# Attention and spectral mixing on one core: v of chunks 28 and 29 made batch by batch, and TensorE's work at the end put into its waits for weights

## The chip, the core and the metric

The kernel runs on one core of a Trainium2 chip. The time is the device time of one execution in microseconds (us); before the change the median of three runs was 439.15 us. Five engines work side by side, each through its own list of instructions in order: TensorE (PE in the profile), VectorE (DVE), ScalarE (ACT), GpSimd (POOL) and SyncE (SP). They wait for each other through semaphores. DMAs are issued by GpSimd's and SyncE's queues and carried by 16 DMA engines.

## The reference

Two stages. First, causal attention over 8 batches, 8 heads, 576 positions and 64 features, with a bias from a running sum. Its result is `x`, 8 x 576 x 512. Then a spectral mix of `x`, cut to its core:

```
X = rfft(x, axis=1)
Xr, Xi = X.real[:, :64], X.imag[:, :64]
Yr = einsum('bmd,mde->bme', Xr, w_r) - einsum('bmd,mde->bme', Xi, w_i)
Yi = einsum('bmd,mde->bme', Xr, w_i) + einsum('bmd,mde->bme', Xi, w_r)
y = irfft(Yr + 1j * Yi, n=576, axis=1)
u = x + y
out = u + maximum(u @ w_ch, 0)
```

`w_r` and `w_i` hold 64 matrices of 512 x 512 each in float32: 134 MB together, all read once.

## The kernel before

The weights are read in 32 **chunks**, four groups of 128 input features (`g`) by eight blocks of eight modes (`c`). A chunk has a real and an imaginary half, `ri` 0 and 1, and each half is one buffer of 128 x 8 x 512 in bfloat16, filled by two DMAs that cast on the way. The last half, the imaginary one of chunk 31, comes in four smaller pieces. GpSimd issues these DMAs (L245), far ahead of their use, as soon as a buffer is free. At most eight of its DMAs are under way.

The first 24 chunks are multiplied between the steps of the attention, the last eight (group 3, chunks 24 to 31, `c` = 0 to 7) behind it. In that last part the code is one straight list, and every engine works through it in the order in which it is written. Nothing reorders it.

- `modes(g, c)` (L479) multiplies one chunk: eight matmuls with the real weights, eight with the imaginary ones. With `meanwhile={2: f}` it calls `f` between the two halves, so that other work of TensorE stands there. For group 3 VectorE adds the sum of the earlier groups (L503) and leaves `yb`: 128 rows (8 modes, real and imaginary, of 8 batches), 512 columns.
- `y_transposed` (L696, copy on ScalarE L698) transposes `yb`; `y_times_wch` (L704, cast on VectorE L708) multiplies it with `w_ch` and leaves `vb`, which is `v = Y @ w_ch`.
- `yv` holds `y` and `v` for the inverse transform, modes on the partitions, batches apart. `spread` (L514) moves the rows of one chunk there with a DMA on SyncE's queue, 128 KB within the core's memory. `gather_round` (L721) does it without a DMA: matmuls that take one batch's columns from the transposed `y` (`which` 0: times the identity, gives `y`; `which` 1: times `w_ch`, gives `v`), and copies from PSUM into `yv` (L732), on ScalarE for `v` and on VectorE for `y` unless said otherwise.
- `work` does the next of the early products of `x` with `w_ch`: `x_transposed` (L663, copies L667) of a pair of output tiles, and `keep` (L676), which multiplies the pair transposed before and has ScalarE put the result aside (L536). `late[-1]` is the last such pair, number 17.
- `x_times_wch` (L676) begins the sums `z` of pairs 0 and 1, `add_y` (L764) and `add_last` (L775) add the inverse transforms to them, `first_u` (L794) begins `u` of pair 0. `add_y(..., slice(0, GK))` reads `yv` of chunks 24 to 29, `add_last` takes chunks 30 and 31 as they come.
- Behind chunk 31 the list of steps from L943 on makes the outputs: sums, ReLU on ScalarE, additions on VectorE and GpSimd, and 20 DMAs to `out`.

In the part that the change touches, TensorE's order before is: chunk 27; three rounds of the gather for chunks 24 to 27 with a `work` behind the third, the fourth round, the last `keep` of a `work`; chunk 28, its transposes, its `v`; chunk 29's real half, its imaginary half, the transposes of `x` for pairs 17 and 0, the transposes of `y`, `z` of pair 0, the transposes of `x` for pair 1, `v`, the gather of `y` for chunks 28 and 29; chunk 30's real half, `keep` of pair 17, its imaginary half, `z` of pair 1 with the transposes of `y` between, `v`; `z` of pair 0 with `yv`; chunk 31.

PSUM has eight banks of 128 x 512 float32: four for `z`, two in `upool` (for the transposes of `x` and a part of the gather, later for `u` of pair 0), two in `auxpool` (for `modes`, the transposes of `y`, `v` and the rest of the gather).

Of the kernel before, what the change touches and what calls it, by code (L numbers as in the profile page):

```python
# [19 lines left out]
def kernel(  # L20
# [20 lines left out]
    NG = DM // P  # L41
# [6 lines left out]
    NCK = NM // MC  # L48
# [207 lines left out]
    for n in range(N):  # L256
# [4 lines left out]
        while nt < min(w // 2, len(wq)):  # L261
            i = ring_of(nt)
# [208 lines left out]
    def modes(g, c, meanwhile=None):  # L471


        ps = auxpool.tile([P, DM], FP32, name="yp", tag="aux")
        cols = xs[g % 2].rearrange("p q k h r b m -> p q k (h r b) m")

        def product(ri, q_, cg):
            k0 = HP if ri == 1 and c == 0 and cg == 0 else 0
            nc.tensor.matmul(  # L479
                ps[32 * cg : 32 * cg + 32, :],  # L480
                cols[k0:, q_, 1 - ri, :, c * MC // 2 + cg],
                wt[(g, c, ri)][cg // 2][k0:, 2 * (cg % 2) + q_, :],
                start=(ri == 0 and q_ == 0), stop=(ri == 1 and q_ == 1),
                tile_position=(k0, 32 * cg), skip_group_check=True,
            )

        for x in range(4):
            ri, y = divmod(x, 2)
            if meanwhile and x in meanwhile:
                meanwhile[x]()  # L490
            for z in range(4):
                if meanwhile:
                    product(ri, z // 2, 2 * y + z % 2)
                else:
                    product(ri, y, z)
        if g == 0:
            nc.vector.tensor_copy(out=y_acc[:, c, :], in_=ps)
        elif g < NG - 1:
            nc.vector.tensor_tensor(out=y_acc[:, c, :], in0=ps, in1=y_acc[:, c, :], op=ALU.add)  # L499
        else:  # L500
            yb = spool.tile([P, DM], FP16, name="y_sb", tag="y")
            for cols in halves if c == NCK - 1 else [slice(0, DM)]:
                nc.vector.tensor_tensor(  # L503
                    out=yb[:, cols], in0=ps[:, cols], in1=y_acc[:, c, cols], op=ALU.add
                )
            if c >= NCK - 1:
                spread(c, 0, yb)
            return yb
# [140 lines left out]
    xts, zs = {}, {}  # L649
# [7 lines left out]
    def x_transposed(i):  # L657
        xts[i] = xt_sb[len(xts) % 3]
        for x, (b, T) in enumerate(pairs[i]):
            ps = upool.tile([P, DT, P], FP32, name="xt_ps", tag="u")  # L660
            for rows, bb, ident in parts(b, T):
                for dt in range(DT):
                    nc.tensor.matmul(  # L663
                        ps[:, dt, rows], x_all[: rows.stop - rows.start, dt, bb, T, :],
                        ident, start=True, stop=True, skip_group_check=True,
                    )
            nc.vector.tensor_copy(out=xts[i][:, x], in_=ps)  # L667
# [4 lines left out]
    def x_times_wch(i, last, xx=(0, 1)):  # L672
        for x in xx:
            start_z(i, x)
            for dt in range(DT):
                nc.tensor.matmul(  # L676
                    zs[i, x], xts[i][:, x, dt, :], wch_sb[:, dt, :],
                    start=(dt == 0), stop=(last and dt == DT - 1), skip_group_check=True,
                )

    def keep(i):
        x_times_wch(i, True)
        j = late.index(i)
        kept_place(i, places[j])
        for x in range(2):
            keep_product(i, x, zs.pop((i, x)))
# [3 lines left out]
    NY = NCK // 2  # L690
    yt_first = finpool.tile([P, DT, NY, P], FP16, name="yt_first")

    def y_transposed(yb, c=NCK):
        ps = auxpool.tile([P, DT, P], FP16, name="yt_ps", tag="aux")
        for dt in range(DT):
            nc.tensor.transpose(ps[:, dt, :], yb[:, bass.ts(dt, P)], ident16h)  # L696
        yt = yt_first[:, :, c % NY, :] if c < NCK - 2 else spool.tile([P, DT, P], FP16, name="yt_sb", tag="yt")
        nc.scalar.copy(out=yt, in_=ps)  # L698
        return yt

    def y_times_wch(c, yt):
        vp = auxpool.tile([P, DM], FP32, name="v_ps", tag="aux")
        for dt in range(DT):
            nc.tensor.matmul(  # L704
                vp, yt[:, dt, :], wch_sb[:, dt, :], start=(dt == 0), stop=(dt == DT - 1)
            )
        vb = spool.tile([P, DM], FP16, name="v_sb", tag="v")
        nc.vector.tensor_copy(out=vb, in_=vp)  # L708
        if c < NCK - 2:
            spread(c, 1, vb)  # L710
        return vb

    def gather_round(c0, c1, b0, which, pool):

        n = 2 * MC * (c1 - c0)
        ng = P // n
        ps = pool.tile([P, DM], FP32, name="g_ps", tag="u" if pool is upool else "aux")
        for dt in range(DT):
            op = yt_first[:, dt, c0 % NY : c0 % NY + c1 - c0].rearrange("p c (x b) -> p (c x) b", b=B)
            for g in range(ng):  # L720
                nc.tensor.matmul(  # L721
                    ps[n * g : n * g + n, :] if which else ps[n * g : n * g + n, bass.ts(dt, P)],
                    op[:, :, b0 + g],
                    wch_sb[:, dt, :] if which else ident16h,
                    start=(dt == 0 or not which), stop=(dt == DT - 1 or not which),
                    tile_position=(0, n * g), skip_group_check=True,
                )

        def copies(engine=None):
            copy = {"v": nc.vector.tensor_copy, "s": nc.scalar.copy}[engine or ("s" if which else "v")]  # L730
            for g in range(ng):
                copy(out=yv[2 * MC * c0 : 2 * MC * c1, b0 + g, which, :], in_=ps[n * g : n * g + n, :])  # L732

        return copies
# [3 lines left out]
    def work():  # L738

        if not order_z and not ahead:  # L740
            return
        if order_z:
            i = order_z.pop(0)
            x_transposed(i)
            ahead.append(i)
        if len(ahead) == 2 or not order_z:
            i = ahead.pop(0)
            keep(i)
# [8 lines left out]
    GK = P - 2 * MC * NX  # L757

    def add_y(dst, i, which, rows=slice(0, P), start=False, xx=(0, 1)):

        for x in xx:
            b, T = pairs[i][x]
            for r, bb, _ in parts(b, T):
                nc.tensor.matmul(  # L764
                    dst[x][r, :], G_sb[rows, bass.ds(T * P, r.stop - r.start)],
                    yv[rows, bb, which, :], start=start, stop=True, skip_group_check=True,
                    tile_position=(0, r.start),
                )

    def add_last(dst, i, yb, cols=slice(0, DM), c=NX - 1, xx=(0, 1)):  # L770

        for x in xx:
            b, T = pairs[i][x]
            for r, bb, _ in parts(b, T):
                nc.tensor.matmul(  # L775
                    dst[x][r, cols], Gx_sb[:, c, bass.ts(T, P)] if T < NF else Gt_sb[:, bb, c], yb[:, cols],
                    start=False, stop=True, skip_group_check=True, tile_position=(0, r.start),
                )
# [64 lines left out]
    def z_of(i):  # L843
        return [zs[i, x] for x in range(2)]

    for c in range(NCK - 2):
        yb = modes(NG - 1, c)
        for x in range(TAKE[c] - 1):
            work()
        if c == NCK - 3:  # L850
            x_transposed(late[-1])
            x_transposed(0)
        yt = y_transposed(yb, c)
        if TAKE[c]:
            work()
        if c >= NY:
            if c == NCK - 3:
                x_times_wch(0, False)
                x_transposed(1)
            y_times_wch(c, yt)  # L860
            if c == NCK - 3:
                for x in range(2):
                    gather_round(NY, NCK - 2, 4 * x, 0, upool)("sv"[x])
        elif c == NY - 1:
            for x, pool in enumerate((auxpool, upool, auxpool, auxpool)):
                for which in (1, 0):
                    gather_round(0, NY, 2 * x, which, pool)()
                if x >= 2:
                    work()
    assert not order_z and not ahead  # L870
    c = NCK - 2
    yb6 = modes(NG - 1, c, {2: lambda: keep(late[-1])})
    x_times_wch(1, False, (0,))
    yt = y_transposed(yb6)
    x_times_wch(1, False, (1,))
    vb6 = y_times_wch(c, yt)


    def first_u():
# [7 lines left out]
    spread(c, 0, yb6)  # L887
    spread(c, 1, vb6)

    def first_z(i):  # L890
        add_y(z_of(i), i, 1, slice(0, GK))
        add_last(z_of(i), i, vb6, c=0)

    first_z(0)
    yb = modes(NG - 1, NCK - 1, {2: lambda: first_z(1), 3: first_u})

    yt = spool.tile([P, DT, P], FP16, name="yt_sb", tag="yt")
    for x in range(2):
# [88 lines left out]
```

## Time and profile before

| | us |
|---|---|
| runs, median (lowest to highest of three) | 439.15 (438.69 to 439.77) |
| the profiled execution | 439.68 |
| its span | 437.9 |
| TensorE matmuls busy | 342.2 (78%) |
| VectorE, ScalarE, GpSimd busy | 251.8, 227.8, 172.5 |
| mean granted TensorE clock | 0.915 |

The span is the time from the first to the last record of the profile; the profiled execution took 1.78 us more. The page cuts the span into 40 slices of 10.9 us and shows for each the busy share of an engine and of the 16 DMA engines. The share of DMA in windows can go over 1, since packets overlap on an engine. In a timeline, what stands in brackets is the time that the engine was idle before the row, and what ended it. 61,424 packets of the span went through GpSimd's queue (81.28 MB as written to the core), 6,938 through SyncE's (11.14 MB, of them 9.4 MB outputs).

### The profile page before, as it was taken

To read this page: it belongs to the slowest core of one execution; us is meant where nothing else is said; L and a number is where in the kernel's file an instruction comes from. 1 tells how busy PE (TensorE), PEld (TensorE's weight loads), DVE (VectorE), ACT (ScalarE), POOL (GpSimd) and SP (SyncE) were. 2 spreads that over 40 slices of the span, in tenths; PEclk is the share of its full clock that TensorE was granted. 3 is DMA by queue.
4 is the path that set the end of the run, shared out by engine and by line. 5 is a ranking of instruction groups with operands and counts; after the bars stand their busy time and mean duration, and the time that the engine had idled before them with its cause. 6 is when DMAs were issued, how large, how long until landed. Compare 5 with 4: busy or idle time off the path is not lost. (4 is left out here: it accounts for less than half of the span.)

```text
span 437.9 us, 10586 instructions
## 1 busy us (share of the span) xinstructions
PE 342.2 (78%) x4409; PEld 204.0 (47%) x4409; DVE 251.8 (57%) x572; ACT 227.8 (52%) x424; POOL 172.5 (39%) x258
## 2 busy tenths in 40 slices
PE   1598989899894977992937557789997987778995
PEld 1366666466562534651615234555553544342441
DVE  7657777657773545771624335566655543471796
ACT  1386887267662724770724224465661343430795
POOL 6555444444344434333344324434222222210493
PEclk9998999989998879896986957999998898999998
DMA  9999999999999999999999999999999999996698
GB/s 163 207 205 206 205 206 207 208 210 206 207 205 207 209 207 210 207 209 209 205 209 208 210 208 209 207 210 207 211 211 211 212 211 210 210 215 131 193 380 339
DMA packets 68409, 93.09 MB, mean 213 GB/s; under 512 B 25278, under 2 KB 27066, under 8 KB 68362
## 3 DMA queue, kind: packets, MB, share of 16 engines
q0 software_dynamic: 61424, 81.28, 105.1%
q1 hardware_dynamic: 6938, 11.14, 7.2%
q8 instruction: 34, 0.56, 0.5%
q14 instruction: 13, 0.11, 0.1%
HBM read 163.37 MB, written 9.51 MB: 395 GB/s over the span
## 5 line engine op out<-in xcount | busy, mean ns | idle before, releaser
L406 ACT ACTIVATE p_sb<-sc_ps,cumt_sb 128x576 f16<-128x576 f32 (+1 forms) x256 | 141.9, 635 | 22.2 <-PE sc_ps L398 21.7
L398 PE MATMUL sc_ps<-qt,kt 128*128 128x512 bf16 (+2 forms) x384 | 78.3, 317 | 6.9 <-ACT kt L360 5.6
L245 POOL DMA_DIRECT2D v<-in_v_dram x72 | 51.3, 713 | 61.9 <-DMA w_sb<-in_moe_w_r_dram 14.9
L245 POOL DMA_DIRECT2D w_sb<-in_moe_w_i_dram x62 | 38.4, 620 | 90.1 <-PE yp L479 30.2
L360 DVE COPY qt<-tr_ps 64x576 bf16<-64x576 bf16 x64 | 47.8, 746 | 40.0 <-PE tr_ps L356 40.0
L479 PE MATMUL yp<-w_sb,xs 128*32 128x512 bf16 (+1 forms) x480 | 42.7, 433 | 29.6 <-DMA w_sb<-in_moe_w_i_dram 27.7
L356 PE MATMUL tr_ps<-ident,qk 64*64 64x64 bf16 x1152 | 34.4, 205 | 32.3 <-DVE kt L360 14.0
L245 POOL DMA_DIRECT2D w_sb<-in_moe_w_r_dram x60 | 37.3, 622 | 52.2 <-DMA w_sb<-in_moe_w_r_dram 34.1
L398 PEld LDWEIGHTS <-kt 128*128 128x128 bf16 x384 | 38.6, 106 | 35.8 <-ACT kt L360 13.3
L392 PE MATMUL sc_ps<-negm,ident 128*128 128x256 bf16 x256 | 54.4, 298 | 0.0
L356 PEld LDWEIGHTS <-qk 64*64 64x64 bf16 x1152 | 26.5, 118 | 50.0 <-DVE kt L360 19.5
L377 ACT ACTIVATE p<-sc_ps,cumt 128x64 f16<-128x64 f32 x32 | 10.0, 313 | 74.9 <-PE sc_ps L373 74.9
L434 PE MATMUL av_ps<-v,p_sb 128*128 128x65 f16 x1024 | 44.7, 198 | 1.8 <-DVE x_all L444 0.7
L360 ACT COPY kt<-tr_ps 64x576 bf16<-64x576 bf16 x32 | 22.8, 714 | 40.5 <-DVE qt L360 39.9
L434 PEld LDWEIGHTS <-p_sb 128*128 128x128 f16 x1024 | 38.1, 100 | 9.5 <-DVE x_all L444 5.4
L469 DVE CAST xs<-ft_ps 64x128 bf16<-64x128 f32 x128 | 36.7, 287 | 6.7 <-PE ft_ps L459 5.4
L439 DVE TENSOR_REDUCE den<-av_ps 128x5 f32<-128x10 f32 x64 | 10.9, 170 | 51.5 <-PE av_ps L434 50.5
L479 PEld LDWEIGHTS <-xs 128*32 128x32 bf16 (+1 forms) x512 | 17.6, 146 | 47.5 <-DMA w_sb<-in_moe_w_i_dram 29.1
L444 DVE TENSOR_TENSOR x_all<-av_ps,rcp 128x320 f16<-128x320 f32 x64 | 31.5, 492 | 2.2
L499 DVE TENSOR_TENSOR y_acc<-yp,y_acc 128x512 f32<-128x512 f32 x16 | 11.1, 692 | 29.5 <-PE yp L479 28.9
L536 ACT COPY z<-z_ps 128x512 f32<-128x512 f32 x22 | 12.9, 585 | 22.8 <-PE z_ps L565 14.2
L459 PE MATMUL ft_ps<-Ff_sb,x_all 128*64 128x192 f16 (+1 forms) x320 | 23.9, 262 | 1.0 <-DVE x_all L444 1.0
(112 smaller groups left out, 442.5 us busy)
## 6 DMA issues: line engine op xcount, KB each, us to landing
w_sb<-in_moe_w_r_dram POOLq DMA_DIRECT2D x60, 512.0 KB, 13.4
w_sb<-in_moe_w_i_dram POOLq DMA_DIRECT2D x55, 512.0 KB, 13.1
out_dram<-r_w SPq DMA_DIRECT2D x16, 512.0 KB
v<-in_v_dram POOLq DMA_DIRECT2D x72, 64.0 KB, 11.1
qk<-in_q_dram POOLq DMA_DIRECT2D x15, 288.0 KB, 11.9
qk<-in_k_dram POOLq DMA_DIRECT2D x15, 288.0 KB, 13.2
x_all<-in_moe_w_r_dram POOLq DMA_DIRECT2D x4, 512.0 KB, 8.8
w_sb<-in_moe_w_i_dram POOLq DMA_DIRECT2D x3, 384.0 KB, 12.7
```

The source lines that it names most:

```text
L245: nc.gpsimd.dma_start(out=dst, in_=src)
L356: nc.tensor.transpose(ps[rows, r, :], src[rows, r, :], ident16[rows, rows])
L360: copy(out=to[:, :, :, half * RH : half * RH + RH], in_=ps[HP * i : HP * i + HP].rearrange("d r (h p) -> d h p r", h=2),)
L392: nc.tensor.matmul(ps[:, bass.ds(w * S, W)], ident16, negm[:, bass.ts(r, W)], start=True, stop=False, skip_group_check=True,)
L398: nc.tensor.matmul(ps[:, c0 : c0 + i1 - i0], keys[:, w, r, :], qh[:, i0:i1], start=False, stop=True, skip_group_check=True,)
L406: nc.scalar.activation(out=pt[:, poff[x] : poff[x] + S - w * W], in_=ps[:, w * S : (w + 1) * S - w * W], func=ACTF.Exp, bias=cumt_sb[:, x, ...
L434: nc.tensor.matmul(ps[:, I, r : r + NCH], lhsT, rhs, start=(i == 0), stop=(i == len(todo) - 1), skip_group_check=True,)
L444: nc.vector.tensor_tensor(out=x_all[:, g, b, :, D * h : D * h + D], in0=ps[:, :, 1 : NCH], in1=rcp.unsqueeze(2).to_broadcast([P, NT, D]), ...
L459: nc.tensor.matmul(ps[HP * q_ : HP * q_ + HP].rearrange("p h f -> p (h f)"), x_all[:nT, g, b, T, q_::2], Ff_sb[:nT, T, :], start=(T == 0), ...
L469: nc.vector.tensor_copy(out=xs[g % 2][HP * h : HP * h + HP, q_, :, h, :, b, :], in_=a)
L479: nc.tensor.matmul(ps[32 * cg : 32 * cg + 32, :], cols[k0:, q_, 1 - ri, :, c * MC // 2 + cg], wt[(g, c, ri)][cg // 2][k0:, 2 * (cg % 2) + ...
L536: nc.scalar.copy(out=z1s[i][:, xx], in_=z)
```

## The change

It touches the last part alone.

- Chunk 28 comes one step sooner: the last `work` of the gather now stands behind chunk 28's products. `v` of chunk 28 is no longer made by `y_times_wch`.
- The three transposes of `x` (pairs 17, 0, 1) stand between chunk 29's real and imaginary halves. Behind them come `keep` of pair 17, the transposes of `y`, and one half of `z` of pair 0.
- `y` and `v` of chunks 28 and 29 both go through `gather_round`, four batches in a round: the first round ahead of chunk 30, the second between chunk 30's two halves, with its copies behind `v` of chunk 30. The two DMAs of `spread` for their `v` are gone.
- Between chunk 30's halves stand also the other half of `z` of pair 0 and both halves of pair 1. `add_y` of pair 0 comes directly behind chunk 30.

```diff
-    for c in range(NCK - 2):
+    for c in range(NCK - 3):
         yb = modes(NG - 1, c)
         for x in range(TAKE[c] - 1):
             work()
-        if c == NCK - 3:
-            x_transposed(late[-1])
-            x_transposed(0)
+        if c == NY:
+            work()
         yt = y_transposed(yb, c)
         if TAKE[c]:
             work()
-        if c >= NY:
-            if c == NCK - 3:
-                x_times_wch(0, False)
-                x_transposed(1)
-            y_times_wch(c, yt)
-            if c == NCK - 3:
-                for x in range(2):
-                    gather_round(NY, NCK - 2, 4 * x, 0, upool)("sv"[x])
-        elif c == NY - 1:
+        if c == NY - 1:
             for x, pool in enumerate((auxpool, upool, auxpool, auxpool)):
                 for which in (1, 0):
                     gather_round(0, NY, 2 * x, which, pool)()
-                if x >= 2:
+                if x == 2:
                     work()
     assert not order_z and not ahead
+    c = NCK - 3
+    yb = modes(NG - 1, c, {2: lambda: [x_transposed(i) for i in (late[-1], 0, 1)]})
+    keep(late[-1])
+    yt = y_transposed(yb, c)
+    x_times_wch(0, False, (0,))
+    for which in (1, 0):
+        gather_round(NY, NCK - 2, 0, which, upool)()
     c = NCK - 2
-    yb6 = modes(NG - 1, c, {2: lambda: keep(late[-1])})
-    x_times_wch(1, False, (0,))
+    gathered = []
+
+    def first_x():
+        x_times_wch(0, False, (1,))
+        x_times_wch(1, False)
+        gathered.extend(gather_round(NY, NCK - 2, 4, which, upool) for which in (1, 0))
+
+    yb6 = modes(NG - 1, c, {2: first_x})
+    add_y([zs[0, x] for x in range(2)], 0, 1, slice(0, GK))
     yt = y_transposed(yb6)
-    x_times_wch(1, False, (1,))
     vb6 = y_times_wch(c, yt)
+    for copies in gathered:
+        copies()
...
-    def first_z(i):
-        add_y(z_of(i), i, 1, slice(0, GK))
-        add_last(z_of(i), i, vb6, c=0)
-
-    first_z(0)
-    yb = modes(NG - 1, NCK - 1, {2: lambda: first_z(1), 3: first_u})
+    def second_z():
+        add_y(z_of(1), 1, 1, slice(0, GK))
+        add_last(z_of(1), 1, vb6, c=0)
+
+    add_last(z_of(0), 0, vb6, c=0)
+    yb = modes(NG - 1, NCK - 1, {2: second_z, 3: first_u})
```

## The prediction, made before the changed kernel ran

> **What bounds the kernel now.** I read the page's slices first: the DMA row stands at 9 from the first slice to the thirty-sixth, so the kernel streams weights until about 404 us. Then I cut the end into stages (busy time of each engine by window; the last two columns are the mean busy share of the 16 DMA engines and GB/s):
>
> ```profile
> 378.00:380.00 2.00, 0.76 (x12) 0.23 (x4) 0.69 (x1) 0.34 (x1) 0.36 (x1) 1.00 1.13 212
> 382.00:384.00 2.00, 0.37 (x8) 0.21 (x8) 0.06 (x1) 0.00 (x0) 0.81 (x3) 1.00 1.11 207
> 386.00:388.00 2.00, 1.78 (x16) 0.95 (x14) 1.43 (x3) 0.58 (x1) 0.59 (x1) 1.00 1.12 232
> 394.00:396.00 2.00, 2.00 (x18) 0.94 (x18) 0.69 (x1) 0.33 (x2) 0.00 (x0) 1.00 1.11 223
> 402.00:404.00 2.00, 1.93 (x10) 0.57 (x10) 0.00 (x0) 0.00 (x0) 0.00 (x0) 1.00 0.22 40
> 406.00:414.00 8.00, 7.86 (x50) 3.57 (x51) 5.27 (x8) 6.28 (x14) 2.78 (x3) 1.00 0.60 167
> 414.00:436.00 22.00, 18.86 (x87) 7.52 (x85) 18.60 (x17) 19.06 (x38) 15.96 (x13) 0.98 0.99 384
> ```
>
> The DMA engines are full (1.11 to 1.13) until 398; then they run out one after another, and at 402 to 404 a share of 0.22 says that only a few of the 16 still carry weights. From 414 on the output stream fills them again. TensorE, first column, has holes: 0.76 and 0.37 of 2 us. What it waits for stands in the timeline of TensorE (start, length, what, idle time and who ended it):
>
> ```profile
> 383.63 0.66 PE L479 MATMUL yp<-w_sb,xs 128*32 128x512 bf16 x8 [1.70 <-DMA w_sb<-in_moe_w_i_dram]
> ...
> 390.79 0.62 PE L479 MATMUL yp<-w_sb,xs 128*32 128x512 bf16 x8
> ...
> 393.97 0.67 PE L479 MATMUL yp<-w_sb,xs 128*32 128x512 bf16 x8 [0.72 <-DMA w_sb<-in_moe_w_i_dram]
> ...
> 398.06 0.60 PE L764 MATMUL z_ps<-yv,G_sb 96*128 96x512 f16 x2 [0.48 <-DMA yv<-v_sb]
> ...
> 399.50 0.67 PE L479 MATMUL yp<-w_sb,xs 128*32 128x512 bf16 x8 [0.40 <-DMA w_sb<-in_moe_w_r_dram]
> ...
> 404.41 0.65 PE L479 MATMUL yp<-w_sb,xs 128*32 128x512 bf16 x4 [0.47 <-DMA w_sb<-in_moe_w_i_dram]
> ```
>
> The products (L479) that end a wait on a weight DMA are those of the imaginary weights of chunks 29 and 30 and of all of chunk 31. The last quarter of chunk 31 begins at 404.41, and everything behind it hangs on it: `y`, its transposes, `v`, the first results at 409.67, then the outputs up to 437.9, 33.5 us later. So one question decides: does the change move 404.41?
>
> **What feeds the weights.** The last three weight buffers are asked for by GpSimd at 379.64 to 389.30 (its timeline); the first waits until chunk 28's real weights have been used, the last three pieces for landings of older ones. From 369.5 to 379.6 nothing is asked for, and still the DMA engines stay at 1.11 to 1.13: the queue is deep enough. So TensorE being early or late by a microsecond there moves no weight.
>
> **The change, part by part.**
>
> *Two spreads of v fewer.* SyncE's timeline has them behind L514 at 382.09 and near 391. Each moves 128 KB within SBUF over the DMA engines that carry the weights. Their cost shows in half-microsecond windows around 386 to 388 and 394.5 to 397: 221, 238, 242, 227 GB/s and 217, 221, 242, 240, 215, over about 210 otherwise. Above 210 that is 44 and 43 KB; the other 87 and 88 KB of 131 KB each displaced weights. At 210 GB/s that is 0.41 + 0.42 = **0.83 us** off the end of the stream. Bounds: all 262 KB displaced weights, 1.25 us; or they only used turns of engines that ran dry at 398 anyway, 0. I take 0.83, because the whole share is at 1.12 while they land: nobody was idle.
> The Trainium skill (DMA: Bandwidth & Descriptors, Where 436 GB/s comes from) says transfers within SBUF are bound by the fabric at 435 GB/s; by that, an estimate of 262 KB / 435 = 0.60 us, and the forecast would be 0.23 us later. The trace's displacement is larger, and I keep it.
>
> *Chunk 28 earlier.* The last kept product (8 matmuls L676, 375.44 to 377.27) goes behind chunk 28's weights. These then wait for ScalarE's copies of the last gather round, which hold the bank until 376.31: start 376.35 instead of 377.27. The kept product ends at 379.1, the transposes of `y` at 379.4. Gone are chunk 28's wait for ScalarE (0.73) and its 4 matmuls of `v` (1.04): chunk 29's real weights go at 379.45 instead of 381.26. They have landed: the pieces land 2.4 us apart, chunk 29's last imaginary one at 383.6, so its last real one near 378.8. Gain for the end: none, by the paragraph above.
>
> *Transposes of x for three pairs in chunk 29's wait.* Six blocks through two banks, each freed by a VectorE copy. Four took 2.44 us (384.22 to 386.66); two more at 0.62 each make 3.7: 380.05 to 383.75, against 383.63 when the imaginary weights come. Hidden but for 0.1.
>
> *Behind chunk 29's imaginary weights* (383.75 to 384.35): keep 1.75, transposes of `y` 0.3, z of pair 0 (4 matmuls) 0.9, up to 387.3, when ScalarE's copy of `y` is ready too (two kept halves, then it: 0.59 each from 385.3). Then `v` and `y` of batches 0 to 3: 16 matmuls of 32 columns are not in the trace with 512 outputs; chunk 28's 16 products of 128*32 took 1.09, the 64-wide gather 0.98 for 8, so 1.96 for 16 at worst. I take 1.05, the same shape. With 0.36 for `y`: 388.75. Chunk 30's real weights need their last landing, near 389.1 (GpSimd's wait ends then): 389.1 to 389.7.
>
> *In chunk 30's wait:* three z halves 2.65, second gather round 1.4: 393.75. The imaginary weights, one displaced spread sooner, come at 393.55. So TensorE is 0.2 late there (1.1 if the gather takes 1.96), before 393.97 all the same.
>
> *Behind them:* `add_y` of pair 0 (0.44) fits beside VectorE's sum (0.69); transposes, copy, `v`, cast as before: ready near 398.2, before 398.3. The wait of 0.48 for the spread at 398.06 is gone, but chunk 31's real weights, 399.50 less 0.83 = 398.67, end last. The second round's copies stand behind the cast: 4 x 0.69 on VectorE to 401.0. The next to need those banks is `first_u`, near 401.65. Cover 0.6 us; gone, it costs what exceeds it.
>
> *Engines:* TensorE 8 matmuls of `v` less, 32 narrow ones more, 2.08 against 2.10: nothing. ScalarE gets 4 copies more (2.3 us), VectorE 4 more and two casts fewer (1.4), all between 387 and 401, where both have holes. The outputs after 404.41 read nothing that comes later than before.
>
> **Sum.** 404.41 becomes 403.58. The profiled execution took 439.68 (span 437.9 and 1.78 around), 0.53 above the median of the runs, 439.15. 439.68 - 0.83 = 438.85, less 0.53: **438.3**. A measurement of this kernel can tell about 0.3%, 1.3 us, from no change, so this counts as no change.
>
> **Rivals.**
>
> *TensorE becomes late (slower).* From 383.75 to 394.3 it now has no hole left. The granted clock (third column from the right) fell once near here, behind a stretch where TensorE was busy 1.19 of 4 us:
>
> ```profile
> 362.00:366.00 4.00, 1.19 (x16) 0.44 (x12) 0.69 (x1) 0.52 (x2) 1.22 (x2) 1.00 1.13 212
> 366.00:370.00 4.00, 3.72 (x28) 2.49 (x30) 1.38 (x2) 1.38 (x3) 1.22 (x2) 0.60 1.13 211
> ```
>
> At half clock every 3.4 us cost 1.7. Slack behind chunk 30 is about 1.5 us (TensorE's waits of 0.40, 0.73 and 0.47 for chunk 31's pieces), so it decides once TensorE is over 1.5 us late at 394: two such windows (3.4), or one (1.7) and the gather at 1.96 a round (0.9 x 2 = 1.8), are 3.5 late, 2 at the end. 438.3 + 2 = **440.3**. Against it: 378 to 384, busy 2.76 of 6 us, kept clock 1.00, and the change fills just these holes.
> The Trainium skill (TensorE: Matmul & The Clock Gate, What's actually happening) has the clock halved after an idle window of about 3.4 us and full after a busy one; by it a TensorE without holes keeps its clock and this rival loses chance. The trace agrees at 366 to 370; no run shows the new order.
>
> *The spreads cost nothing.* The engines that finish last (0.22 at 402 to 404) lag because they are slow; if the spreads went through the others' spare turns, the end stays: **439.15**. For it: the ramp from 398 to 404.4 is 6.4 us long, against 0.83 for two spreads. Against: a spread of 128 rows over 16 engines gives the late ones work too.
>
> *The stream gains more (faster).* All 262 KB displaced weights (1.25 us), and chunk 30's imaginary request, 0.9 us sooner after a gap of 10 us, spares the early engines a hole (207 GB/s at 382 to 384, 2% under the rest, and as much in three more windows: 0.2 us). 1.45 us: **437.7**.
>
> **Chances.** Forecast 0.45, more gain 0.2, nothing 0.17, TensorE late 0.18. Of the forecast 0.07 lies beyond 0.3% by the spread of the runs (438.69 to 439.77): faster 0.27, within 0.55, slower 0.18. Range: from the rival of more gain, less half the runs' spread, 437.1, to the slower one, 440.3.
>
> **What would show it.** In the profile after: two DMAs of `yv<-v_sb` instead of four; no windows above 215 GB/s from 384 to 397; the last L479 block near 403.6; imaginary weights of chunk 29 and 30 with waits on DMA near zero; real ones of chunk 31 still waiting for DMA. I am wrong if the last block is not earlier, if it waits for something other than a weight DMA, if the granted clock falls under 1 between 380 and 409, or if the time from that block to the end is not about 33.5 us.

## The result

The changed kernel takes 440.63 us (median of 22 runs, 439.37 to 442.95), the kernel before 439.38 beside it (438.67 to 440.83). The ratio is 1.0030, with a 95% interval of 1.0017 to 1.0043: 1.3 us slower, where 0.8 us faster was forecast. The profiled execution took 439.51 with a span of 437.7, one of the shortest of the 22, and a little shorter than the profiled execution before. So its span alone says nothing; its parts do. Of all the executions below, one of e6's twelve took 951.76 us, and e6's ratio leaves it out.

The same stages in the changed kernel's profile (busy time by engine, then granted clock, DMA share and GB/s):

```profile
378.00:380.00 2.00, 1.44 (x22) 0.84 (x20) 0.87 (x2) 1.05 (x2) 1.82 (x3) 1.00 1.11 209
382.00:384.00 2.00, 1.98 (x13) 0.57 (x12) 1.50 (x3) 0.00 (x0) 0.59 (x1) 0.52 1.12 210
386.00:388.00 2.00, 1.92 (x21) 1.03 (x23) 0.00 (x0) 1.07 (x2) 0.00 (x0) 1.00 1.11 206
394.00:396.00 2.00, 1.04 (x8) 0.54 (x8) 0.26 (x1) 1.21 (x3) 0.00 (x0) 1.00 1.12 209
402.00:404.00 2.00, 0.98 (x7) 0.31 (x6) 0.61 (x2) 0.00 (x0) 0.00 (x0) 1.00 0.01 1
406.00:414.00 8.00, 7.94 (x46) 3.26 (x45) 6.38 (x8) 7.39 (x15) 4.48 (x4) 1.00 0.61 207
414.00:436.00 22.00, 17.15 (x80) 6.78 (x78) 16.89 (x16) 17.34 (x35) 14.27 (x12) 0.94 0.94 364
```

The change did what it says. The bumps of the spreads are gone (206 and 209 GB/s where 232 and 223 stood; 218 from 384 to 386, where 24 KB of instruction fetches fall), and TensorE's holes at 378 and 382 are filled, the second one at half clock (0.52). The last row looks like a slower output stage, 364 GB/s instead of 384. But everything at the end stands 1.71 us earlier in this profile, and in a window that is shifted by as much the outputs run as before, at 383:

```profile
412.29:434.29 22.00, 18.86 (x87) 7.53 (x85) 18.60 (x17) 19.05 (x38) 15.97 (x13) 0.98 0.99 383
```

TensorE's timeline:

```profile
382.08 1.09 PE L479 MATMUL yp<-w_sb,xs 128*32 128x512 bf16 x8
...
392.88 0.62 PE L479 MATMUL yp<-w_sb,xs 128*32 128x512 bf16 x8
...
397.78 0.68 PE L479 MATMUL yp<-w_sb,xs 128*32 128x512 bf16 x8
...
400.14 0.65 PE L479 MATMUL yp<-w_sb,xs 128*32 128x512 bf16 x4 [0.70 <-DMA w_sb<-in_moe_w_i_dram]
...
402.70 0.65 PE L479 MATMUL yp<-w_sb,xs 128*32 128x512 bf16 x4 [0.50 <-DMA w_sb<-in_moe_w_i_dram]
```

The imaginary halves of chunks 29 and 30 no longer wait for a DMA; the last quarter of chunk 31 still does. It comes 1.71 us sooner than in the profile before, but chunk 27's last imaginary products stand 1.54 sooner too (362.20 against 363.74), ahead of everything that the change touches: weights drift by that much between executions. So two measures are used from here on, which leave that drift out:

- the **stretch**, from chunk 27's last imaginary products to chunk 31's last quarter: 40.67 us before, 40.50 after. Where one row holds all 16 products of chunk 27, it counts from the ninth;
- the **drain**, from the end of SyncE's last output issue to the end of the span: 2.72 before, 4.23 after.

The drain is where the lost time stands. SyncE's last issues in the profile before and the end of its DMA stream, in half-microseconds:

```profile
432.99 2.19 SPq L841 DMA_DIRECT2D out_dram<-r_w  x3
```

```profile
436.00:436.50 0.50, 0.00 (x0) 0.00 (x0) 0.00 (x0) 0.00 (x0) 0.00 (x0) 0.50 1.03 401
436.50:437.00 0.50, 0.00 (x0) 0.00 (x0) 0.00 (x0) 0.00 (x0) 0.00 (x0) 0.50 0.04 12
```

And in the changed kernel:

```profile
431.27 2.20 SPq L841 DMA_DIRECT2D out_dram<-r_w  x3
```

```profile
434.50:435.00 0.50, 0.00 (x0) 0.00 (x0) 0.00 (x0) 0.00 (x0) 0.00 (x0) 0.50 0.65 246
435.00:435.50 0.50, 0.00 (x0) 0.00 (x0) 0.00 (x0) 0.00 (x0) 0.00 (x0) 0.50 0.06 25
435.50:436.00 0.50, 0.00 (x0) 0.00 (x0) 0.00 (x0) 0.00 (x0) 0.00 (x0) 0.50 0.06 25
436.00:436.50 0.50, 0.00 (x0) 0.00 (x0) 0.00 (x0) 0.00 (x0) 0.00 (x0) 0.50 0.04 16
```

Before, the 16 engines end together: a share of 1.03, then 0.04. After, fifteen end by 435.0, and a share of 0.06 goes on into the window up to 436.5. That is 1/16: **one** DMA engine still has output to carry, and the kernel ends with it.

What held that engine back is in a line of the page that the prediction never read, the queue of instruction fetches. Before and after, over the whole span (packets, MB, share of 16 engines):

```profile
q8 instruction: 34, 0.56, 0.5%
```

```profile
q8 instruction: 35, 0.57, 0.5%
```

One fetch more, of 0.57 MB / 35 = 16 KB. And by window, in the DMA queues of 404 to 414 us before, and of 399 to 401 and 426 to 428 us after:

```profile
q8 instruction: 1, 0.02, 1.1%
```

```profile
q8 instruction: 1, 0.02, 2.8%
...
q8 instruction: 1, 0.02, 4.8%
```

Before, the last fetch falls between the weights and the outputs, where the DMA engines are half idle (a share of 0.46 from 408 to 410), and none follows after 414. After, one falls into the last microseconds of the weights and the next into the middle of the outputs. One packet on one engine: 4.8% of 16 engines over 2 us is 1.5 us of that engine, about its lag at the end. The length alone does not decide: the fetch before took 1.7 us (1.1% over 10 us), and no engine lagged at the end. The profile does not name the engines; that the lag comes with the fetch rests on the experiments below. The other instruction queue, q14, has one packet of 8 KB between 418 and 421 in every profile, before as after, and so cannot make the difference.

### The profile page after: what moved, and what is told of

It is laid out like the page before. It is cut to its first block, busy times and chain, and to the rows that moved or that the text cites. A ratio compares the mean times of both kernels' runs of the same rounds, so it can differ in the third digit from the quotient of the medians.

```text
span 437.7 us, 10638 instructions
## 1 busy us (share of the span) xinstructions
PE 343.6 (78%) x4433; PEld 205.5 (47%) x4433; DVE 253.4 (58%) x574; ACT 229.9 (53%) x428; POOL 172.6 (39%) x258
## 5 line engine op out<-in xcount | busy, mean ns | idle before, releaser
L398 PE MATMUL sc_ps<-qt,kt 128*128 128x512 bf16 (+2 forms) x384 | 77.1, 313 | 8.0 <-ACT kt L360 6.5
L479 PE MATMUL yp<-w_sb,xs 128*32 128x512 bf16 (+1 forms) x480 | 44.0, 445 | 27.6 <-DMA w_sb<-in_moe_w_i_dram 25.2
L444 DVE TENSOR_TENSOR x_all<-av_ps,rcp 128x320 f16<-128x320 f32 x64 | 31.5, 492 | 2.2
```

The source lines that it names most:

```text
L398: nc.tensor.matmul(ps[:, c0 : c0 + i1 - i0], keys[:, w, r, :], qh[:, i0:i1], start=False, stop=True, skip_group_check=True,)
L444: nc.vector.tensor_tensor(out=x_all[:, g, b, :, D * h : D * h + D], in0=ps[:, :, 1 : NCH], in1=rcp.unsqueeze(2).to_broadcast([P, NT, D]), ...
L479: nc.tensor.matmul(ps[32 * cg : 32 * cg + 32, :], cols[k0:, q_, 1 - ri, :, c * MC // 2 + cg], wt[(g, c, ri)][cg // 2][k0:, 2 * (cg % 2) + ...
```

## The experiments

Three theories stood after the first comparison: the clock (TensorE, emptied at 394 to 398, falls to half clock in some executions), the stream (the weights end later), and the outputs (the drain). The first four kernels ran together.

**e1, the changed kernel again.**

> The changed kernel once more, for a second profile and ten times beside the kernel before. Clock theory: emptying 394 to 398 (TensorE busy 2.26 of 4 us instead of 3.57) lets the granted clock fall in some executions during chunk 31 and the chain behind it, so times are wider spread than before's and about 1.3 us longer; a slow profile shows the clock under 1 between 397 and 409 and the stretch from the last L479 block to the last issued output over 31 us (30.8 in both profiles so far). Stream theory: the last block itself is late, over 41 us behind chunk 27's last imaginary block (40.5 after, 40.7 before). Output theory: both are unchanged and only the last outputs drain later (4.2 us from the last issue to the end after, 2.7 before).

440.81 us, ratio 1.0032 (1.0015 to 1.0049). The drain is 4.20 again. The stretch is 41.59 (chunk 27's imaginary products begin with their weight load at 362.62, the first row below; the next two rows are windows), and here the clock theory has its case. The granted clock is low from 398 to 402, and the last quarter follows without a wait for a DMA:

```profile
362.62 0.22 PEld L479 LDWEIGHTS <-xs 128*32 128x32 bf16 x8 [0.39 <-DMA w_sb<-in_moe_w_i_dram]
...
398.00:400.00 2.00, 1.36 (x6) 0.32 (x9) 1.96 (x3) 1.12 (x2) 0.00 (x0) 0.63 0.74 138
400.00:402.00 2.00, 2.00 (x16) 0.54 (x8) 1.39 (x3) 0.00 (x0) 0.00 (x0) 0.52 0.49 93
...
399.58 1.09 PE L479 MATMUL yp<-w_sb,xs 128*32 128x512 bf16 x8
...
402.22 0.65 PE L479 MATMUL yp<-w_sb,xs 128*32 128x512 bf16 x4
...
404.21 0.65 PE L479 MATMUL yp<-w_sb,xs 128*32 128x512 bf16 x4
```

So TensorE can be the late one, in some executions. The drain is there without it.

**e2, the kernel before again.**

> The kernel before once more, for a second profile: the ratio is 1.000. All theories: 40.7 us from chunk 27's last imaginary block to the last block, 30.8 from there to the last issued output. Output theory: under 3 us from the last issue to the end; if it is over 4 here too, that drain is chance and not the change's.

439.43 us, ratio 1.000 (0.9987 to 1.0013); stretch 41.23, drain 2.73. The drain is the kernel's and not chance; the stretch varies by half a microsecond.

**e3, z of pair 1 back around chunk 30's transposes.**

```diff
     def first_x():
         x_times_wch(0, False, (1,))
-        x_times_wch(1, False)
...
     add_y([zs[0, x] for x in range(2)], 0, 1, slice(0, GK))
+    x_times_wch(1, False, (0,))
     yt = y_transposed(yb6)
+    x_times_wch(1, False, (1,))
     vb6 = y_times_wch(c, yt)
```

> The changed kernel with the two halves of z of pair 1 (8 matmuls, 1.9 us) put back around the transposes of y of chunk 30, as before; all else as changed. Clock theory: TensorE is busy 3.5 of 4 us in 394 to 398 again, the slow executions go, and the time is 0.2 to 0.8 us under the kernel before (438.6 to 439.2), spread as before's. Stream and output theories: no difference from the changed kernel, about 440.6.

440.43 us, ratio 1.0021 (1.0007 to 1.0035), drain 4.06. TensorE is busy again from 394 to 398, and the kernel is still slower than before. But its profiled execution had the half clock in just these microseconds, and its last quarter, too, begins without a wait for a DMA:

```profile
396.00:398.00 2.00, 2.00 (x9) 1.00 (x8) 0.00 (x0) 0.52 (x1) 0.00 (x0) 0.50 0.99 185
...
404.77 0.65 PE L479 MATMUL yp<-w_sb,xs 128*32 128x512 bf16 x4
```

So e3 does not rule the clock out. What does, as the main cause, is e8 and e9 below: they keep the changed order and lose the slowdown.

**e4, two spreads put back.**

```diff
         if c == NY:
             work()
+            spread(NCK - 1, 0, yb)
...
     keep(late[-1])
+    spread(NCK - 1, 1, yb)
     yt = y_transposed(yb, c)
```

> The changed kernel with two DMAs of 128 KB put back at about the times of the removed ones (y of chunks 28 and 29, into rows of yv that chunk 31 fills later); nothing waits for them. If a spread displaces weights, as the prediction has it, the last block comes 0.8 us later and the time is 0.8 over the changed kernel (441.4). If the spreads cost nothing, it is the same, 440.6, and two fewer spreads were never a gain. If the lost spreads themselves made the changed kernel slow (the engines out of step), it falls back to 439.4.

440.89 us, ratio 1.0038 (1.0024 to 1.0052), drain 4.0. So the missing spreads did not make the kernel slow: with two of them back it is no faster. Against e1 they cost 0.1 us by the medians, inside the noise of both.

All kernels with the changed order had the long drain, and all had the 35th fetch behind 414. What they share, beside the order, is a list of TensorE's that is 48 instructions longer: 4,433 matmuls and as many weight loads, instead of 4,409. The next four change that length, e5 in the kernel before.

**e5, the kernel before with 48 instructions more.**

```diff
             for q_ in range(2):
-                nc.tensor.matmul(
-                    ps[HP * q_ : HP * q_ + HP].rearrange("p h f -> p (h f)"),
-                    x_all[:nT, g, b, T, q_::2], Ff_sb[:nT, T, :],
+                for cols in [slice(0, 96), slice(96, 192)] if n in (9, 10) or (n == 11 and T < 2) else [slice(0, 192)]:
+                    nc.tensor.matmul(
+                        ps[HP * q_ : HP * q_ + HP].rearrange("p h f -> p (h f)")[:, cols],
+                        x_all[:nT, g, b, T, q_::2], Ff_sb[:nT, T, cols],
...
```

> The kernel before with 24 of its Fourier matmuls (L459, in three steps of the attention) cut into two of half the width: the same result, and TensorE's list 48 instructions longer, as long as the changed kernel's; nothing of the change is in it. Instruction theory: the profile of the changed kernel has one DMA of 16 KB more on the instruction queue, and it falls into the output stream (one between 414 and 438 us, none before); one of the 16 engines then lags, and the end drains 4 us behind the last issue instead of 2.7. By it this kernel shows the same: one fetch after 414, a drain of about 4.1, 1.2 us over the kernel before (440.6). Order theory (the loss comes from where the work stands): no difference, 439.4, drain 2.7. The halves themselves cost at most 24 x 0.2 us in a part where DMA is the bound.

441.33 us, ratio 1.0051 (1.0031 to 1.0070; six runs). Nothing of the change is in this kernel, and it loses at least as much as the changed one. Its DMA queues from 414 on hold the fetch, and the end of its stream (windows of 1 us) has the lone engine; the drain is 4.18:

```profile
q8 instruction: 1, 0.02, 0.4%
```

```profile
436.00:437.00 1.00, 0.00 (x0) 0.00 (x0) 0.00 (x0) 0.00 (x0) 0.00 (x0) 0.50 0.50 191
437.00:438.00 1.00, 0.00 (x0) 0.00 (x0) 0.00 (x0) 0.00 (x0) 0.00 (x0) 0.50 0.06 25
```

Its stretch is 41.51, over both of before's. There, too, a fetch falls into the last microseconds of the weights (401 to 403), but chunk 31's last quarter waits only 0.27 us for its weights, and the clock was half from 384 to 391; so the longer stretch is not shown to be the fetch's.

**e6, the changed kernel with 64 instructions fewer.**

```diff
-        for T in range(NT):
+        TS = 1 if 9 <= n < 13 else NT
+        for T in range(TS):
...
```

> The changed kernel with 32 Fourier matmuls left out (four of the five position tiles in four steps of the attention), so TensorE's list is 64 instructions shorter, 15 below the kernel before's; all of the change stays. Instruction theory: no fetch after 414, drain 2.7, and the time falls by 1.3 to 1.5 us to 439.2, or to 438.5 if the two spreads saved also count once the fetch is out of the way. Order theory: stays at 440.6 with a drain of 4.1.

439.15 us, ratio 0.9991 (0.9980 to 1.0002), drain 2.79, no fetch after 414, stretch 39.77. The slowdown is gone with the whole change in place. The kernel leaves out four of five position tiles in four steps of the transform, so it also does less work; e8 answers that. The short stretch is not all gain: from the last quarter to SyncE's last issue it takes 31.5 us instead of 30.8, with a wait of TensorE's for a DMA `yv<-v_sb` (0.56 us at 411.73). e7 has the same, and why is open.

**e7, y of chunks 28 and 29 by spread.**

```diff
         if c == NY:
             work()
+            spread(c, 0, yb)
...
     keep(late[-1])
+    spread(c, 0, yb)
...
-    for which in (1, 0):
-        gather_round(NY, NCK - 2, 0, which, upool)()
+    gather_round(NY, NCK - 2, 0, 1, upool)()
...
-        gathered.extend(gather_round(NY, NCK - 2, 4, which, upool) for which in (1, 0))
+        gathered.append(gather_round(NY, NCK - 2, 4, 1, upool))
```

> The changed kernel with y of chunks 28 and 29 moved by two spread DMAs instead of 32 gather matmuls: TensorE's list is 64 instructions shorter than the changed kernel's, with two DMAs of 128 KB in the weight stream. Instruction theory: no fetch after 414, drain 2.7; the time is 1.3 under the changed kernel plus 0.1 (measured for two spreads put back) to 0.8 (predicted): 439.4 to 440.1. Order theory: 440.7 and a drain of 4.1.

439.71 us, ratio 1.0004 (0.9992 to 1.0017), drain 2.70, stretch 40.41. Its list is as short as e6's, with two spreads in the stream: 0.56 us more by the medians.

**e8, the changed kernel with 200 instructions more.** The cut of e5, in ten steps (`if 9 <= n < 20 and n != 16`).

> The changed kernel with 100 Fourier matmuls cut into halves: 200 instructions of TensorE more, which shifts the fetch that falls into the output stream some 200 instructions earlier, to about 408 us, where the DMA engines are nearly idle; the one after it would lie past the end. Instruction theory, in its form that the place of the fetch counts and not their number: drain 2.7, time 439.2 plus at most 0.3 for the halves. In its form that each fetch costs: 441. Order theory: 440.6 to 441 with a drain of 4.1.

438.95 us, ratio 0.9986 (0.9976 to 0.9997), drain 2.83, stretch 40.20. The list is the longest so far, the fetches are still 35, and the median is the lowest: the last fetch has moved from 427 to 406 to 408 us, ahead of the outputs. From its DMA queues in 404 to 414, and the end of its stream:

```profile
q8 instruction: 1, 0.02, 1.0%
```

```profile
435.00:436.00 1.00, 0.00 (x0) 0.00 (x0) 0.00 (x0) 0.00 (x0) 0.00 (x0) 0.50 1.03 395
436.00:437.00 1.00, 0.00 (x0) 0.00 (x0) 0.00 (x0) 0.00 (x0) 0.00 (x0) 0.50 0.02 4
```

No lone engine. The place of the fetch costs, not the number of instructions or of fetches. The last four kernels ran together again.

**e9, e8 again**, and **e10, e8 with the two spreads of e4.**

> The changed kernel with 200 instructions more once again (100 Fourier matmuls cut into halves, the same result), as the base for the next one: 0.9986 of the kernel before, about 438.9, no instruction fetch after 414 us, drain 2.8. If the first result was luck, 1.000.

> The kernel of e9 with two DMAs of 128 KB put back at about the times of the removed ones (y of chunks 28 and 29 into rows that chunk 31 fills later; nothing waits for them). The price of two spreads with the instruction fetch out of the way: by the prediction 0.83 us over e9 (0.0019); by e7 against e6, 0.56; by e4 against e1, 0.1.

e9: 438.99 us, ratio 0.9999 (0.9988 to 1.0010), stretch 39.79, drain 2.86. The median is e8's; the ratio, taken against the runs beside it, is not under 1 this time. So the changed order with its fetches out of the way is at most a little faster than the kernel before: 0.9986, 0.9999 and e6's 0.9991 average to 0.9992, 0.35 us. e10: 439.61 us, ratio 1.0006 (0.9998 to 1.0015), stretch 41.72. Two spreads cost 0.62 us by the medians and 0.3 by the ratios.

**e11, the changed kernel with 100 instructions more** (the cut in five steps, `if 9 <= n < 14`).

> The changed kernel with 50 Fourier matmuls cut into halves: 100 instructions of TensorE more instead of 200, so the last fetch comes some 150 instructions before the end of its list, near 418 us, early in the output stream instead of late (428) or ahead of it (408). If an engine that lags by a fetch cannot catch up because all 16 are full from 414 on: drain 4.1, 440.6 as the changed kernel. If holes in the output stream let it catch up: drain 2.8 to 3.5, 439 to 440. If it is the number of instructions that costs: 440.9 or more.

439.31 us, ratio 1.0011 (0.9999 to 1.0024). The last fetch falls at 416 to 418, early in the outputs; the drain is 3.59, between the two others. So the engine seems to make up for part of the fetch on the way, as the second answer had it, though the drain is just over its 3.5.

**e12, the kernel before with 112 instructions fewer** (four of five position tiles left out in seven steps, `TS = 1 if 9 <= n < 16 else NT`).

> The kernel before with 56 Fourier matmuls left out (four of the five position tiles in seven steps of the attention): a shorter list, by 112 instructions, and less work. Its last fetch, ahead of the output stream before (408), then comes about 146 instructions before the end, near 418 us, in the stream. If the place of the fetch decides and the engine cannot catch up: drain 4.1 and 1.2 us over the kernel before, 440.6, though the kernel does less. If number or work counted: 439.4 or less, drain 2.7.

439.92 us, ratio 1.0021 (1.0009 to 1.0033), drain 3.19: a shorter list with less work, and slower, since its last fetch has slid back from 408 to 416 to 418. The expected 1.2 us was too much; like e11 it points to a partial catch-up. Its stretch, 41.81, is also on the long side. In its profiled execution the granted clock was 0.50 from 400 to 402, and the last quarter begins at 404.02 without a wait for a DMA, so there TensorE was late as well.

## Why the prediction was wrong

**The step that failed** is the line on the engines: "TensorE 8 matmuls of `v` less, 32 narrow ones more, 2.08 against 2.10: nothing." The busy times are right (each narrow round of `v` took 1.09 us, 1.05 was taken). But 24 matmuls net are 48 instructions with their weight loads, and those were priced by their time alone. They moved every later fetch of TensorE's list: the last but one into the weights' last microseconds, the last into the outputs. By e5 alone that costs 0.5% (2.2 us; 1.4 to 3.1 by its interval), by the changed kernel against e8 and e9 0.37% (1.0030 less 0.9993, 1.6 us). Of this 1.3 to 1.5 us is the drain, seen in every profile with the late fetch (4.0 to 4.23) and in none without one after 414 (2.70 to 2.86). The rest is open. The stretches point the same way (41.51 in e5 against 40.67 and 41.23; 40.50 and 41.59 in the changed kernel against 39.77, 40.20 and 39.79 with the fetches moved). But they do not show weights held up by the fetch: the changed kernel's 40.50 is below both of before's, and in e1 the last quarter waited for no weights at all.

**The main term is probably too large.** Two spreads fewer were put at 0.83 us, from what they displaced in the GB/s of the profile. The runs have 0.1 (e4 against e1), 0.56 (e7 against e6, which also swaps `y`'s gather), and 0.62 or 0.3 (e10 against e9). All lie below 0.83, but by the intervals of the ratios each carries 0.6 to 1 us of noise, so none of them excludes it alone. The reading itself was soft: in the same view, windows without a spread range from 205 to 221 GB/s (388 to 391), so some 10 GB/s of what was counted above 210 in a window can be chance. The estimate of 0.60 from the Trainium skill (DMA: Bandwidth & Descriptors, Where 436 GB/s comes from) lies nearer to these runs than the reading of the windows. The whole change without its late fetches brought 0.35 us by the average of e6, e8 and e9 (e6 does less work, e8 and e9 have split matmuls), not 0.83.

**The order on TensorE came as worked out.** Counted from chunk 27's last imaginary products: chunk 28 at 12.81 (worked out: 12.61), chunk 29's real half at 15.90 (15.71), its imaginary half at 19.88 (20.0). From 382 on the clock was half for 3.4 us (0.52 and 0.63 over 2 us each), so chunk 30's real half came at 26.28 instead of 25.4 and its imaginary half at 30.68 instead of 30.0. Chunk 31's first half then waited for VectorE's cast of `v` and no longer for its weights, which the prediction had the other way round; the two waits behind it absorbed that (0.70 and 0.50 for DMA).

**The claim on the clock failed.** That filled holes keep the clock at 1.00 was wrong for the profiled execution: it fell at 382, inside the filled wait, where 32 small matmuls stand apart by VectorE's copies (1.36 of 2 us busy). In e3 and e9, with the same list there, it stayed at 1.00 through that wait, so it is a matter of the execution. The rival "TensorE becomes late" said when this costs, and four profiles show it: e1, e4 and e11 at half clock for some 6.8 us in a row (0.50 from 384 to 388), twice as long as the changed kernel's own profile, and e3 from about 395 to 398. In all four the last quarter begins without a wait for its weights; in the other profiles of the changed order it waits for them, by 0.40 to 0.50 us. What this lateness costs is not measured: e11 has it with a stretch of 40.23. It is a second loss and a likely reason for the wider spread of the runs, which was not tested by itself. That the measured 440.63 lies close to this rival's 440.3 is mostly luck, since 1.3 to 1.5 us of the loss is the drain.

**The tail.** Two of the signs of being wrong came true: the granted clock fell under 1 between 380 and 409, and the time from the last block to the end is not about 33.5 us. It is 35.0, with the same 30.8 us up to the end of the last issue. The second sign is the one that led to the cause.

## What to carry to other kernels

Where DMA engines are full to the end, read the instruction queue's line as well, and ask in which window its last packets fall. An edit that lengthens or shortens one engine's list moves all later fetches; the same work with 200 instructions more was 1.6 us faster here than with none, by the ratios. When an edit costs a microsecond that no busy time explains, test its instruction count alone, with the same number of split instructions in the kernel before. And compare parts of profiles (here from one fixed product to another, and from the last issue to the end), not two spans: the profile of the slower kernel had the shorter one.

## What the runs showed of the hardware that was not expected

- TensorE's list is fetched in pieces of 16 KB (0.57 MB in 35), one packet on one DMA engine, about once in 259 instructions (8,818 matmuls and loads in 34 fetches). In the windows it took that engine 0.9 us (2.8% of 16 over 2 us) while few weights were left, 1.5 us in the full output stream, and 1.7 us at 408, where no engine lagged at the end for it. 200 instructions more moved the last one 19 us earlier (from 427 to 408).
- A fetch of 1.5 us late in the output stream let one engine end 1.3 to 1.5 us after the rest: drain 4.0 to 4.2 with the fetch at 426 to 429, 3.2 to 3.6 at 416 to 418, 2.7 to 2.9 ahead of 414. That the time left to catch up makes the difference is argued from this order and was not tested by itself.
- The Trainium skill (Runtime: NRT & Kernel Launch, Instruction fetch mechanics) has blocks of 16 KiB, 256 instructions, and calls the cost of crossing one mostly hidden. The size agrees with the traces. The cost does not, at the end of a kernel that is bound by DMA: e5, whose list is only longer by 48 instructions, measures 1.0051.
